# A fixed list of issue orders, DMA transposes and more seven-product batches in a Nystrom attention + MLP kernel

## The chip, the cores and the metric

The kernel runs on one core of a Trainium2 chip. Five engines work side by side, each through its own queue in order: TensorE (PE, with its weight loads, PEld), VectorE (DVE), ScalarE (ACT), GpSimd (POOL) and SyncE (SP, which only issues DMAs here). The metric is the device time of one execution in microseconds. The time before is the median of three runs, 268.52 us (267.44 to 269.39). A profile is one execution of the program, and its span runs from the first to the last instruction.

## The reference

Inputs q, k, v have shape (8 batches, 8 heads, 576 positions, 64). Attention goes through 32 landmarks, each the mean of 18 positions; the result is layer-normed over 512 features and sent through a two-layer MLP (512 to 2048 to 512) with a residual:

```python
q_lm = q.reshape(B, H, m, S // m, D).mean(axis=3)      # m = 32
k_lm = k.reshape(B, H, m, S // m, D).mean(axis=3)
A, Bm, C = sm(q, k_lm), sm(q_lm, k_lm), sm(q_lm, k)    # sm: softmax of scaled products
Z = Bm.transpose(0, 1, 3, 2) / (norm1(Bm) * norminf(Bm) + 1e-06)
for _ in range(6):
    Z = 2 * Z - Z @ Bm @ Z
attn = A @ Z @ C @ v                                    # heads side by side: x, (8, 576, 512)
xn = (x - mean(x)) / sqrt(var(x) + 1e-06) * g_ln
out = x + maximum(xn @ w_ch1, 0.0) @ w_ch2
```

## The kernel before

**Tiling.** A unit is four heads of one batch: a tile of 128 partitions by 1152 values (`stg` as loaded in fp32, `nat` in fp16). Batch 0 is done by `attention0`; the other batches run through `attention2` in the sets (1), (2), (3, 4), (5, 6), (7), whose six iterations of Z share matmuls and banks.

**Turning q and k (batches 1 to 7).** `Coming.turn` makes the transposed tile `xT` with one DVE transpose of 32x32 blocks on pairs of fp16 values (28 of them). The scores therefore run on cells of 32x32 (`scores_k`, `scores_q`: `psec`, `psea`), and the exponentials of the k side, `ec`, are transposed once more on DVE (`ecT`). Landmark sums come in three ways: on TensorE with `pairs16` (`tot`, then the DVE transpose `lmt`), by DVE reductions of `xT` (`add_up`, into `part`), or by sums on POOL (`asum`, `s16`, then `sT`); a matmul with `spread16` brings `part` into the form `lm`. Batch 0 is turned by TensorE with an identity (`pst`, copied to `xT`), and its scores run on 128x64 cells (`psc`) and 64x32 cells (`psa`).

**First layer.** `First.products` multiplies the per-head matrices `zt` with w1 (`m16`, fp16), and `chunk` makes 128 hidden features for 576 positions: four matmuls of 288 columns into one of two double-bank slots (`psh`, tag `p2`), then a ReLU on ACT or DVE into `hT`. The layer norm's mean is taken out of w1 itself: `less` holds minus the mean over features; batches 0 and 1 add it after the product (`copies`, with `less` and `total`), then `center_w1` adds it into w1 for the rest.

**Second layer.** Blocks of 128 positions: 16 matmuls of 512 columns each, then one DVE addition into `xblk` with the norm's factor `rstd`, and two stores. For batches 4 to 7 (`FAST = 4`) four blocks are done by seven products in place of eight (`seven_products`): 112 matmuls of 256 columns in place of 64 of 512, with mixed weights (`w2_mix`, 16 subtractions on POOL), eight mixes of `hT` per batch on DVE (`mix_ahead`) and more, narrower additions.

**What sets the order.** Each engine's order is that in which the program emits. A planner, `Clock`, estimates at build time when each engine and tile is free (`note`, `took`); `run` takes the next ready one of five streams (attentions, totals, first layers, rows of batch 0, second layers), and `help_out` puts loads, casts, mixes, measures and stores between them. A table `AFTER` holds some steps back by count. `Ring` gives out buffers in turn; loads go through six `stg` slots on SP's queue. The first part (batch 0 up to its `zt`, loads and scaling of w1, loads of w2 and of batch 1) is written out by hand.

Of the kernel before, what the change touches and what calls it, by code (L numbers as in the profile page):

```python
# [16 lines left out]
P = 128  # L17
# [3 lines left out]
def kernel(  # L21
# [40 lines left out]
    NEVER = 1e12  # L62

    def name_of(x):
        return x.tensor.name if hasattr(x, "tensor") else x.name

    parted, mixed_, parted_w1 = {}, set(), set()

    def key_of(ap):

        return keys_of(ap)[0]

    def keys_of(ap):
        n = name_of(ap)
        if n not in parted:
            return [n]
        at = [ap.offset]
        for step, k in list(ap.ap)[1:]:
            if step >= parted[n]:
                at = [o + step * i for o in at for i in range(k)]  # L80
        if n in mixed_:
            return [f"{n}:{o // parted[n]}:{int(o % parted[n] >= 256)}" for o in at]
        return [f"{n}:{o // parted[n]}" for o in at]

    class Clock:


        WAY = 55.0
        OVERLAP = {"Activation": 110, "DVE": 80, "Pool": 30}

        def __init__(self):
            self.free = dict.fromkeys(("PE", "DVE", "Activation", "Pool", "SP"), 0.0)
            self.wrote, self.used, self.begun = {}, {}, {}
            self.small, self.lanes, self.wire = False, {}, 0.0
            self.cells, self.count, self.mark, self.fetched, self.ahead = [], 0, 95, 0.0, 0.0
            self.loads, self.pool = [], []
            self.free['PE'], self.issued = 1500.0, 0

        def share(self, span=3400.0):

            now = self.now()
            return sum(c for t, c in self.cells if t > now - span) / span

        def now(self):
            return max([self.free["PE"]] + list(self.lanes.values()))

        BLOCK, LEAD = 128, 16

        def both(self, *at):
            return max(max(at), ps2.next("p2", 2))  # L110

        def calm(self, n):

            return self.fetched if self.count + n + (20 if late() else 0) >= self.mark else 0.0

        def at(self, *tiles):
            return max([self.wrote.get(name_of(t), (0.0, ""))[0] for t in tiles] + [0.0]) + self.WAY

        def at_key(self, ap):
            return self.wrote.get(key_of(ap), (0.0, ""))[0] + self.WAY  # L120

        def idle_key(self, ap):
            n = key_of(ap)
            return max(self.wrote.get(n, (0.0, ''))[0], self.used.get(n, (0.0, ''))[0]) + self.WAY

        def idle(self, *tiles):

            return max([max(self.wrote.get(n, (0.0, ""))[0], self.used.get(n, (0.0, ""))[0],
                            self.begun.get(n, 0.0)) for n in map(name_of, tiles)] + [0.0]) + self.WAY

        def took(self, i, e, n, m):
            op = type(i).__name__
            if e == "Activation":
                return 300 if n < 8 else 190 + (1.07 if name_of(i.outs[0].bass_ap).startswith("ec_") else 0.79) * n
            if e == "Pool":
                if n == 1024 and name_of(i.outs[0].bass_ap) in mixed_:
                    return 2080
                if "Ptr" in op:
                    return 100 + 1.29 * n
                return 100 + 0.92 * n if "Copy" in op else 280 + 1.76 * n  # L140
            if n == 1152 and "Copy" in op:
                return 760
            if "Stats" in op:
                return 690 if m > 100 else 180
            if n >= 512 and (n == 576 or op == 'InstTensorCopy'):
                return 100 + 1.13 * n
            if n == 1024:
                last = max([b for a, b in self.pool if a <= self.ready < b] + [0.0])
                queued = 1000 if self.free["Pool"] > self.ready else 690
                return max(queued, last - self.ready + 560)  # L150
            if n == 256 and "Ptr" in op and name_of(i.outs[0].bass_ap).startswith("xblk"):
                return 480
            if "Transpose" in op:
                return 110 + 1.15 * n
            return 140 + 1.15 * max(n, m if "Reduce" in op else 0)

        def note(self, i):
            e = str(i.engine).rsplit(".", 1)[-1]
            outs = [a.bass_ap for a in i.outs if hasattr(a, "bass_ap")]
            ins = [a.bass_ap for a in i.ins if hasattr(a, "bass_ap")]  # L160
            size = [[k for _, k in a.ap] for a in outs + ins]
            count = []
            for dims in size:
                n = 1
                for k in dims[1:]:
                    n *= k
                count.append(n)
            reads = [n for a in ins for n in keys_of(a)]
            writes = [n for a in outs for n in keys_of(a)]
            ready = 0.0  # L170
            for n in reads:
                t, who = self.wrote.get(n, (0.0, e))
                if who != e or e != "PE":
                    ready = max(ready, t + (self.WAY if who != e else 0.0))
            for n in writes:
                for t, who in (self.wrote.get(n, (0.0, e)), self.used.get(n, (0.0, e)),
                               (self.begun.get(n, 0.0), "")):
                    if who != e:
                        ready = max(ready, t + self.WAY)
            if type(i).__name__ == "InstDMACopy":  # L180
                start = max(self.free[e], ready)
                self.free[e] = start + (580 if e == "SP" else 100)
                half_ = size[0][0] == 64 and any(n.startswith("stg") for n in writes)
                self.wire = (max(start + 1650, self.wire)
                             + count[0] * size[0][0] * 4 / (150.0 if half_ else 385.0))
                self.loads = self.loads[-24:] + [(start, self.wire)]
                self.issued += 1
                late_ = 1500 if self.issued <= 4 else 600 + min(2200, 0.8 * (self.wire - start - 1650))
                done = self.wire + late_
                start = done  # L190
            elif e == "PE":
                cols = count[0]
                if self.count == self.mark - self.LEAD:
                    self.ahead = self.now()
                if self.count == self.mark:
                    self.mark += self.BLOCK
                    ready = max(ready, self.fetched)
                    asked = max(self.ahead, self.fetched - 200)
                    behind = max([w for t, w in self.loads if t <= asked] + [0.0])
                    self.fetched = max(asked + 1200, behind + 400) + 2450  # L200
                self.count += 1
                rows_, cols_ = tuple(i.tile_size)
                self.cells.append((self.now(), cols / 2.4 * rows_ * cols_ / 128 ** 2))
                if tuple(i.tile_size) == (128, 128):
                    if self.small:
                        self.free[e] = max(list(self.lanes.values()) + [self.free[e]]) + 100
                        self.small, self.lanes = False, {}
                    start = max(self.free[e], ready)
                    self.free[e] = start + max(cols / (1.2 if start < 5200 else 2.4) + 3, 56)
                    done = self.free[e] + 160  # L210
                else:
                    if not self.small:
                        self.small, self.lanes = True, {}
                        self.free[e] += 95
                    elif self.shape != (rows_, cols_):
                        self.free[e] = max(list(self.lanes.values()) + [self.free[e]]) + 85
                    self.shape = rows_, cols_
                    lane = [(a, c) for a in range(i.tile_position[0], i.tile_position[0] + rows_, 32)
                            for c in range(i.tile_position[1], i.tile_position[1] + cols_, 32)]
                    start = max([self.free[e], ready] + [self.lanes.get(x, 0.0) for x in lane])  # L220
# [1577 lines left out]
```

## Time and profile before

| | us | how to read it |
|---|---|---|
| runs | 268.52, 267.44, 269.39 | device time of three executions |
| profiled execution, span | 266.1 | first to last instruction; the page does not give this execution's own time, and the median of the runs lies 2.4 above the span |
| granted TensorE clock | 0.999 | full speed throughout |
| chain, TensorE after 45 us | 45 to 262.6 | products of first and second layer, almost without a break |
| start | 0 to 22 | q, k, v and w1 land; batch 0's attention on TensorE between waits |
| last matmul to end | 262.6 to 266.1 | last addition, last store |
| DMA share, 22:45 / 45:85 / 85:150 / 150:240 | 1.05 / 0.93 / 0.60 / 0.17 | loads of weights, then of later batches; stores at the end |
| DVE busy in the same stretches | 16.3 of 23 / 36.9 of 40 / 53.0 of 65 / 67.7 of 90 | |
| ACT busy | 19.3 / 29.2 / 52.2 / 62.0 | |
| POOL busy | 18.8 / 32.1 / 53.6 / 16.1 | casts, sums, mixes of w2; nearly idle after 175 us |

Busy shares are averages over stages with different limits. [...]

### The profile page before, as it was taken

To read this page: it belongs to the slowest core of one execution; us is meant where nothing else is said; L and a number is where in the kernel's file an instruction comes from. 1 tells how busy PE (TensorE), PEld (TensorE's weight loads), DVE (VectorE), ACT (ScalarE), POOL (GpSimd) and SP (SyncE) were. 2 spreads that over 40 slices of the span, in tenths; PEclk is the share of its full clock that TensorE was granted. 3 is DMA by queue.
4 is the path that set the end of the run, shared out by engine and by line. 5 is a ranking of instruction groups with operands and counts; after the bars stand their busy time and mean duration, and the time that the engine had idled before them with its cause. 6 is when DMAs were issued, how large, how long until landed. Compare 5 with 4: busy or idle time off the path is not lost.

```text
span 266.1 us, 8332 instructions
## 1 busy us (share of the span) xinstructions
PE 256.5 (96%) x3442; PEld 167.9 (63%) x3442; DVE 202.8 (76%) x461; ACT 175.2 (66%) x337; POOL 133.6 (50%) x160
## 2 busy tenths in 40 slices
PE   7889998999999999999999999999999999999994
PEld 7644754466545554546655465578878765788883
DVE  2657873899999979788984986989684599819762
ACT  2578997378868896589797559787377654871000
POOL 5288788999729387499999934500000042000000
PEclk9999999999999999999999999999999999999999
DMA  7999999999976996766611120110060006100606
GB/s 253 380 396 389 388 386 393 317 343 306 354 237 172 388 363 187 207 174 198 200 43 39 34 52 2 42 43 0 2 158 0 2 4 160 43 0 2 158 17 183
DMA packets 23566, 46.68 MB, mean 175 GB/s; under 512 B 2404, under 2 KB 2664, under 8 KB 23528
## 3 DMA queue, kind: packets, MB, share of 16 engines
q1 hardware_dynamic: 23048, 45.49, 53.3%
q10 hardware_dynamic: 480, 0.66, 0.7%
q8 instruction: 27, 0.44, 0.7%
q14 instruction: 11, 0.09, 0.1%
HBM read 36.70 MB, written 9.44 MB: 173 GB/s over the span
## 4 chain that ended last, share of the span: by engine, by line
PE 78%; DMA 11%; DVE 3%; POOL 3%; issue 2%; SPq 1%; ACT 1%; POOLq 0%; DVEq 0%
PE bank L304 51%; PE psh L304 21%; DMA stg<-in_v_dram 6%; DMA wstg<-in_moe_w_ch_dram 3%; DMA stg<-in_q_dram 2%; PE pscv L304 1%; POOL natv L298 1%; PE psd L304 1%; DVE xblk L298 1%; PE psec L304 1%; PE psm L304 1%; PE psea L304 1%; POOL w L298 1%; SPq L313 1%; DVE st L298 1%
## 5 line engine op out<-in xcount | busy, mean ns | idle before, releaser
L304 PE MATMUL bank<-w,hT 128*128 128x512 f16 (+3 forms) x528 | 111.7, 335 | 1.2 <-issue 0.8
L298 ACT ACTIVATE hT<-psh 128x576 f16<-128x576 f32 x119 | 73.6, 654 | 21.9 <-PE psh L304 21.0
L304 PEld LDWEIGHTS <-hT 128*128 128x128 f16 x656 | 60.3, 98 | 32.5 <-issue 8.6
L304 PE MATMUL psh<-ea,m 128*128 128x288 f16 x512 | 78.3, 286 | 0.6 <-DVE ea L298 0.3
L304 PEld LDWEIGHTS <-m 128*128 128x128 f16 x512 | 48.8, 97 | 20.2 <-issue 3.7
L298 DVE SCALAR_TENSOR_TENSOR xblk<-bank,rstd,xblk 128x256 f32<-128x256 f32 (+2 forms) x77 | 39.0, 539 | 22.4 <-PE bank L304 22.3
L298 POOL TENSOR_TENSOR ea<-ea,lns 128x576 f16<-128x576 f16 x14 | 18.9, 1371 | 60.4 <-ACT lns L298 54.6
L298 POOL CAST nat<-stg 128x1152 f16<-128x1152 f32 x21 | 23.8, 1147 | 8.5 <-DVE xT L298 6.4
L298 DVE BATCH_NORM_STATS2 six<-xblk 128x6 f32<-128x512 f32 x36 | 24.2, 673 | 0.9 <-ACT xblk L298 0.9
L298 POOL CAST natv<-stg 128x1152 f16<-128x1152 f32 (+1 forms) x17 | 19.3, 1165 | 9.7 <-DMA stg<-in_v_dram 7.7
L298 DVE STREAM_TRANSPOSE xT<-nat 128x576 uint32<-128x576 uint32 x28 | 21.4, 763 | 0.0
L298 ACT COPY xblk<-bank 128x512 f32<-128x512 f32 (+1 forms) x32 | 18.0, 591 | 4.0 <-PE bank L304 3.7
L304 PE MATMUL bank<-w2mix 128*128 128x256 f16 x128 | 17.1, 273 | 0.0
L304 PE MATMUL bank<-w2mix,hT 128*128 128x256 f16 x128 | 15.8, 273 | 0.0
L298 DVE SCALAR_TENSOR_TENSOR st<-st,bank 128x128 f16<-128x128 f16 (+2 forms) x36 | 11.1, 308 | 5.9 <-PE bank L304 5.7
L298 ACT CAST m<-bank 128x512 f16<-128x512 f32 x18 | 9.9, 586 | 7.5 <-PE bank L304 7.4
L298 DVE TENSOR_REDUCE part<-xT 128x32 f16<-128x576 f16 x20 | 14.6, 744 | 0.2
L298 ACT ACTIVATE lns<-psd 128x576 f32<-128x576 f32 x16 | 10.3, 644 | 6.0 <-PE psd L304 5.9
L304 PE MATMUL bank<-zcbd,ea 128*128 128x256 f16 x80 | 14.1, 273 | 0.0
L298 DVE SCALAR_TENSOR_TENSOR m<-less,zsum,bank 128x512 f16<-128x512 f16 (+1 forms) x18 | 11.5, 682 | 3.0 <-PE bank L304 1.4
L304 PEld LDWEIGHTS <-w2mix 128*128 128x128 f16 x128 | 12.4, 98 | 2.0 <-issue 0.2
L304 PEld LDWEIGHTS <-st 32*32 32x32 f16 x448 | 5.9, 90 | 11.9 <-DVE st L298 8.9
(135 smaller groups left out, 365.9 us busy)
## 6 DMA issues: line engine op xcount, KB each, us to landing
stg<-in_q_dram SPq DMA_DIRECT2D x16, 576.0 KB, 6.3
stg<-in_k_dram SPq DMA_DIRECT2D x16, 576.0 KB, 6.0
out_dram<-xblk SPq DMA_DIRECT2D x66, 128.0 KB, 2.4
wstg<-in_moe_w_ch_dram SPq DMA_DIRECT2D x16, 512.0 KB, 7.3
stg<-in_v_dram SPq DMA_DIRECT2D x10, 576.0 KB, 7.2
stg<-in_v_dram SPq DMA_DIRECT2D x6, 288.0 KB, 6.2
stg<-in_v_dram SPq DMA_DIRECT2D x12, 144.0 KB, 6.0
out_dram<-xblk ACTq DMA_DIRECT2D x4, 128.0 KB, 3.2
```

What stands on the lines that cost most here:

```text
L298: return lambda *args, **kw: keep(getattr(self.engine, op)(*args, **kw))
L304: keep(nc.tensor.matmul(o, l, r, start=start, stop=stop, tile_position=(rb, cb), skip_group_check=(skip or cb != 0)))
L313: keep(queue.dma_start(out=t[:], in_=src[b, 4 * u:4 * u + 4].rearrange("(r e) (t j) d -> (e t) r j d", e=2, j=NJ)))
```

## The change

The planner, its `Clock`, the streams and `help_out` are gone. The program now first records all work as operations (`Op`: one instruction, or a run of matmuls), 1656 of them, numbered in the order of the source; then it issues them in the order of a literal list, `ORDER`, with the engine of each movable operation from a second literal, `BY` (A, D or P for ACT, DVE, POOL). Buffers are given out at issue, from fixed slots (`Place`); two psum double banks and four banks as before, `nat` 4 slots (6 before), `e` 12 (14), `mix` 3 and `stg` 6.

- Batches 2 to 7 are turned by a DMA on SP's queue (`turn_by_dma`, 24 in all, 128 x 1152 fp16 each); batch 1 is turned by TensorE as batch 0 is (`BY_PE`). The DVE transposes of `xT`, `ecT`, `sT`, `lmt` and the products with `pairs16` and `spread16` are gone. All scores run on the cells that batch 0 uses (`psc`, `psa`), `psa` of two units together.
- Landmarks: k by POOL sums and a 64-column matmul, q by DVE reductions of the whole `xT` (`qlm`, `HOW`), batch 1 by TensorE.
- `seven_products` for batches 2 to 7; the mixes of `hT` are on DVE or POOL (23 and 25), and each batch uses three `mix` slots.
- Sets are (1), (2), (3), (4, 5), (6, 7). w1 is centred before batch 1's first layer; only batch 0 adds the mean afterwards.
- More casts, ReLUs and scalings may be on DVE or ACT. All loads of v are whole tiles; SP has 70 of the 128 KB stores (66 before).
- Of the hand-written first part the order of loads stays.

```diff
-    class Clock:
...
-    def help_out(hurry=False):
...
-    EARLY = {0: 8}
-    HK, HN, FAST = MCH // 2, DM // 2, 4
...
+    class Op:
+        def issue(self, by):
+            for b in self.bufs:
+                b.place()
+            for ways, args, kw in self.calls:
...
+                    tc.keep_in_program_order(ways(ISSUE[by], *args, **kw))
...
+    def turn_by_dma(n16):
+        t = xT_tile()
+        later("S", lambda e, o, i: e.dma_start_transpose(out=o, in_=i),
+              t, n16.rearrange("p j r d -> p (j r d)"))
+        return t
...
+                xT = [turn_by_pe(t, "AD") if b in BY_PE else turn_by_dma(t) for t in tiles]
...
+    def mix(o, left, right, op):
+        for k in (0, 4):
+            n = ds(k, 4)
+            tt("DP", o[:, n, :], left[:, n, :], right[:, n, :], op)
...
+    SETS = ((1,), (2,), (3,), (4, 5), (6, 7))
+    FAST, BY_PE, TWO = (2, 3, 4, 5, 6, 7), (1,), 2
+    HOW = {(b, nm): "T" if b in BY_PE else "P" if nm == "k" else "D" for b in range(B) for nm in "kq"}
...
+    ORDER = """
+        0-2 14 3-6 9 15 52 17 10 16 18 11 19 55 21 12 20 22-23 58 25 13 24 27 26 28 61 29-30 32 34
...
+    BY = """
+        DADADDPAAAAAADAAAAAADAAADAAAAAADDADAADDADDADDDADADAAADAAAADAAADDAADDDADAADAADPDDPPDPADDP
...
+    for i in order:
+        program[i].issue(by[i])
```

More of the change, by code (lines that the diff above doesn't have):

```diff
@@ L59 @@
     wpool = ctx.enter_context(tc.tile_pool(name="wpool", bufs=1))
[L62 to L83, printed above, removed]
@@ L85 @@
-    class Clock:
[L88 to L220, printed above, removed]
-                    self.lanes.update((x, start + max(cols / 2.4, 30)) for x in lane)
-                    self.free[e] = start + (8 if rows_ == 64 and cols < 128 else 4)
-                    done = self.lanes[lane[0]] + 160
-            else:
-                start = max(self.free[e], ready)
-                self.ready = start
-                done = start + self.took(i, e, count[0], max(count[1:] + [0]))
-                self.free[e] = done - self.OVERLAP[e]
-                if e == "Pool":
-                    self.pool = self.pool[-8:] + [(start, done)]
-                if e == 'DVE' and count[0] == 1024 and writes[0] in parted_w1:
-                    self.free['Pool'] = max(self.free['Pool'], start) + 430
-            for n in reads:
-                self.used[n] = max(self.used.get(n, (0.0, e)), (done, e))
-                if n.startswith("m16") and ":" in n:
-                    self.begun[n[:n.index(":")] + "."] = done
-            for n in writes:
-                self.wrote[n] = max(self.wrote.get(n, (0.0, e)), (done, e))
@@ new lines, with __init__, take @@
+    class Place:
+        def __init__(self, pool, tag, words, slots):
+            self.tag, self.slots = tag, slots
+            self.tiles = [pool.tile([P, words], FP32, name=tag, tag=f"{tag}{i}") for i in range(slots)]
+            self.free = list(range(slots))
+            places[tag] = self
+        def take(self, buf):
+            i = self.free.pop(0)
+            n = 1
+            for d in buf.shape[1:]:
+                n *= d
+            t = self.tiles[i]
+            t = t[0:buf.shape[0], 0:(n if buf.dtype == FP32 else n // 2)]
+            if buf.dtype != FP32:
+                t = t.bitcast(buf.dtype)
+            if len(buf.shape) > 2:
+                names = "abcd"[:len(buf.shape) - 1]
+                spaced = " ".join(names)
+                t = t.rearrange(f"p ({spaced}) -> p {spaced}", **dict(zip(names, buf.shape[1:])))
+            return i, t
@@ new lines, with __init__, take, place @@
+    class Fixed(Place):
+        def __init__(self, tag, tiles):
+            self.tag, self.slots, self.tiles = tag, len(tiles), tiles
+            self.free = list(range(self.slots))
+            places[tag] = self
+        def take(self, buf):
+            i = self.free.pop(0)
+            return i, self.tiles[i][:]
+    class Buf(View):
+        def __init__(self, tag, shape, dtype, name):
+            self.tag, self.shape, self.dtype, self.name = tag, shape, dtype, name
+            self.of, self.chain, self.at, self.uses = self, [], None, 0
+            bufs.append(self)
+        def place(self):
+            if self.at is None and not isinstance(places[self.tag], Turns):
+                self.slot, self.at = places[self.tag].take(self)
+            return self.at
+        def done(self):
+            self.uses -= 1
+            if self.uses == 0 and self.at is not None:
+                places[self.tag].free.append(self.slot)
@@ L431, in load_w1, with e_tile @@
+    def e_tile(shape, name):
+        return Buf("e", shape, FP16, name)
+    less = {}
+    w1_coming, w2_coming = [], []
     def load_w1(i):
         f, half = divmod(i, 2)
-        stg = stage.tile([P, 2, DM], FP32, name="wstg", tag="stg")
-        keep(nc.sync.dma_start(out=stg[:], in_=w1_src[:, 2 * half:2 * half + 2, ts(f, DM)]))
-        w1_coming.append(stg)
-    def scale_w1(i, c, engine):
+        t = Buf("stg", [P, 2, DM], FP32, "wstg")
+        dma(t, w1_src[:, 2 * half:2 * half + 2, ts(f, DM)])
+        w1_coming.append(t)
@@ new lines, with room_for, mean_begun, mean_copied @@
+    hTs = {}
+    def room_for(b):
+        if b < B and b not in hTs:
+            hTs[b] = Buf(f"hT{b % 2}", [P, MCH, S + 64 * (b % 2)], FP16, "hT")
+    def mean_begun(f, psf, c0, c1):
+        for c in range(c0, c1):
+            MM(psf, lesser[:], w1_16[:, c, ts(f, 512)], start=(c == 0), stop=(c == KCH - 1))
+    def mean_copied(f, psf):
+        less[f] = e_tile([P, 512], "less")
+        copy("A", less[f], psf)
+    def center_w1(f):
+        for c in (0, 2):
+            o = w1_16[:, ds(c, 2), ts(f, 512)]
+            tt("D", o, o, less[f][:, None, :].broadcast_to([P, 2, 512]), ALU.add)
@@ new lines, in first_layer, with keep_tail @@
+    def first_layer(l1):
+        two = l1.b >= TWO
+        for m in range(MCH):
+            if two and m % 8 == 0:
+                l1.two_products_of_heads(m // 4)
+            if not two and m % 4 == 0:
+                l1.product_of_heads(m // 4)
+            l1.chunk(m)
+    def keep_tail(b):
+        if b % 2 == 0:
+            room_for(b + 1)
+            copy("P", hTs[b + 1][:, :, 0:64], hTs[b][:, :, S - 64:S])
+    TAIL = {None: ds(0, DM), 0: ds(0, DM - DM // 4), 1: ds(DM - DM // 4, DM // 4)}
@@ L1212, in store @@
+    def store(j, x, cols, last=False):
         for i in range(2):
@@ L1765 @@
     next(a0)
-    run()
-    help_out(True)
+    cut()
+    fixed = len(program)
+    l1, psf = first0[0], {}
+    l1.product_of_heads(0)
+    psf[1] = bank()
+    mean_begun(1, psf[1], 0, KCH)
+    mean_copied(1, psf[1])
+    next(a0)
+    for m in range(MCH):
+        l1.chunk(m)
+        if m in (1, 3):
+            scale_w1(m + 4, 1, "A")
+        if m in (2, 5):
+            f = 2 if m == 2 else 3
+            psf[f] = bank()
+            for c in range(KCH):
+                mean_begun(f, psf[f], c, c + 1)
+                cut()
+            mean_copied(f, psf[f])
+        if m in (1, 4, 7):
+            l1.product_of_heads((m + 2) // 3)
@@ L1771 @@
+    assert sorted(order) == list(range(len(program)))
+    ways = iter("".join(BY.split()))
+    by = [op.by if len(op.by) == 1 else next(ways) for op in program]
+    for i in order:
+        program[i].issue(by[i])
 _INS = ['q', 'k', 'v', 'moe_g_ln', 'moe_w_ch1', 'moe_w_ch2']
```

1901 lines of the change are left out of this document (694 added, 1207 removed), and 38 rows, old and new, of tables (AFTER, ORDER).

## The prediction

> **What bounds the kernel now.** I read the busy times and the chain of waits first.
>
> ```profile
> PE 256.5 (96%) x3442; PEld 167.9 (63%) x3442; DVE 202.8 (76%) x461; ACT 175.2 (66%) x337; POOL 133.6 (50%) x160
> PE 78%; DMA 11%; DVE 3%; POOL 3%; issue 2%; SPq 1%; ACT 1%; POOLq 0%; DVEq 0%
> PE bank L304 51%; PE psh L304 21%; DMA stg<-in_v_dram 6%; DMA wstg<-in_moe_w_ch_dram 3%; DMA stg<-in_q_dram 2%; PE pscv L304 1%; POOL natv L298 1%; PE psd L304 1%; DVE xblk L298 1%; PE psec L304 1%; PE psm L304 1%; PE psea L304 1%; POOL w L298 1%; SPq L313 1%; DVE st L298 1%
> ```
>
> TensorE carries 78% of the chain; DMA has 11%, all of it before 40 us. A busy matmul row overlaps the next one, so 96% does not yet say that TensorE is full. The timeline of TensorE in the middle of the span says it (start, duration, instruction):
>
> ```profile
> 119.82 0.65 PE L304 MATMUL psh<-ea,m 128*128 128x288 f16 x4
> 120.31 0.38 PE L304 MATMUL bank<-w,hT 128*128 128x512 f16 x1
> 120.53 0.38 PE L304 MATMUL bank<-zcbd,ea 128*128 128x256 f16 x2
> ...
> 123.92 0.59 PE L304 MATMUL bank<-w,hT 128*128 128x512 f16 x2
> 124.44 0.41 PE L304 MATMUL bank<-w,zt 64*32 64x512 f16 x8
> 124.67 0.40 PE L304 MATMUL psm<-w,zt 64*32 64x512 f16 x8
> 125.00 0.67 PE L304 MATMUL psh<-ea,m 128*128 128x288 f16 x4
> ```
>
> From start to start, four 288-column products take 0.49 us (122 ns each) and one of 512 takes 0.216 us. That is the price of an instruction here; its own duration includes the pipeline. Two 512s take 0.43 us, yet 124.44 is 0.52 after 123.92: going from 128x128 cells to 64x32 costs 0.09 us. Over the trace the median of such a change of cell shape is 95 ns, and there are 159 of them. With these prices the starts from 22 us to the last matmul at 262.6 us divide into about 222 us of columns, 12.3 us of shape changes, 4.4 us of waits (gaps over 25 ns) and 2 us of crumbs. So TensorE is full from 22 us on, and only fewer columns, fewer changes of shape or those 4.4 us can pay. Before 22 us it waits for loads; from 262.6 to 266.1 lie the last addition and the last store.
>
> Profiled span 266.1 us; the three runs have a median of 268.5, so 2.4 us are added for what lies around the span.
>
> **The change on TensorE, start-to-start prices.** The built instruction streams give the counts.
> - Seven products for batches 2 and 3: out 128 of 512 columns (128 x 0.216 = 27.6), in 224 of 256 (224 x 0.109 = 24.4): -3.2.
> - Landmarks: out 72 products with `pairs16` (56 ns, 4.0) and 10 with `spread16` (1.1); in 36 + 12 of 64 columns (29 ns, 1.4): -3.7.
> - Batch 1 turned by TensorE: 36 transposes at 56 ns: +2.0.
> - Scores of seven batches: out `psec` 224 (4.4), `psea` 224 (3.4), landmark products 112 (0.7). In `psc` 252 at the 20 ns that batch 0's 36 took (5.0), landmark products (0.3), and `psa` in seven pairs. Batch 0's unpaired tile takes 0.5 us, so 14 x 0.5 = 7.0 bounds it above; a pair uses eight different cells at once, 0.213 + 0.027 = 0.24, so 1.7 bounds it below. I take 2.2, near the eight-cell row (`w,zt` x8: 0.23 from start to start). -1.0.
> - Fewer products for `zt`: -0.3. Changes of shape 159 to 171: 12 x 0.095 = +1.1.
>
> Sum -5.1 us. The two unknowns move it from -5.6 to -0.3.
>
> **What else moves.** *DVE.* Sum of durations now 226 us (counts by mean durations; neighbours overlap, hence 202.8 busy). Out: 28 transposes of `xT` (763 ns, 21.4), 20 reductions to `part` (14.6), `ecT` (6.8), `sT` and its reductions (4.9), `lmt` (1.7), nine of the 32 mixes (6.6), 8 `xblk` of 512 (5.8), 8 `m` with `less` (5.9). In: 28 more `xblk` of 256 (476 ns, 13.3), 14 more `hT` (754, 10.5), 10 casts of `nat` and `natv` (760, 7.6), 10 `ea` scalings (288 columns take 524, so 0.95: 9.5), 12 reductions of 1152 columns that no row shows: 576 take 744, so 0.74 if only the output counted and 1.5 by columns; 1.4 taken, 17.0; smaller copies and masks 10.7. Within 1 us of even, and off the path by the cover above: 45 to 85 us runs with DVE at 36.9 of 40 us and PE at 40.0. *ACT* loses (198 to about 181). *POOL* gains: 25 mixes of 1024 (512 columns: 1.15, so 1.1 by the `hT` copy of 1024 to 2.2; 2.2 taken, 55 us), two landmark sums (5.7), less 8 + 7 casts and ten scalings (31): 138 to about 167, still under 0.7 of the span.
>
> *Centring* of w1 (8 x 0.76 us of DVE) comes before batch 1's first layer instead of behind its products; it has TensorE's 15 to 37 us for cover, and beyond it batch 1's products wait.
>
> *SP.* 24 turns are added, each waiting in SP's order for its tile's cast (DVE, ACT or POOL); queued behind it are the next loads and stores. From the first turn on, the casts of those loads stand 4.6 to 11 us of TensorE's columns behind them in the list, against a landing of 6: the shortest have no cover, but the tiles' first TensorE readers come 8 us or more behind their turns. A turn moves 288 KB and no row shows one. Nearest rows:
>
> ```profile
> stg<-in_q_dram SPq DMA_DIRECT2D x16, 576.0 KB, 6.3
> out_dram<-xblk SPq DMA_DIRECT2D x66, 128.0 KB, 2.4
> stg<-in_v_dram SPq DMA_DIRECT2D x6, 288.0 KB, 6.2
> ```
>
> Below: the lone store's 2.4 us. Above: element by element; a packet of 4 bytes takes 9 ns, and 147,456 elements over 16 engines are 83 us. I take 3 to 6, the rows of like size. In the list, a turn of k is issued 12 to 35 us of columns ahead of its TensorE reader, a turn of q 4.4 to 13.5 ahead of DVE's reduction (eight of twelve 6 or more). So 6 us fit nearly all of it, TensorE reads the q tiles later still, and I cost the turns at nothing. [...]
>
> *The list itself.* Of 126 re-uses of a `psh` slot, 52 leave TensorE under 0.95 us of columns to cover one evacuation (0.65 on ACT, 0.75 on DVE, plus the hand-overs); in the new list 17 do, and the median cover grows from 1.09 to 1.80 us. That can win some of the 4.4 us; fuller ACT and DVE at 110 to 130 us of columns (23.5 and 24.3 us of work in 20) can lose as much. I put the waits at no change. Loads to 45 us keep their order, so what is saved there may not count (up to 0.5).
>
> Forecast: 266.1 - 5.1 = 261.0 span, 263.4 us with the 2.4.
>
> **Rivals.**
> *DVE and POOL in each other's way.* The trace speaks for it:
>
> ```profile
> 216.36 0.68 DVE L298 TENSOR_TENSOR w2mix<-hT 128x1024 f16<-128x1024 f16 x1
> 217.16 1.57 DVE L298 TENSOR_TENSOR w2mix<-w2mix,hT 128x1024 f16<-128x1024 f16 x1
> ...
> 216.72 3.16 POOL L298 TENSOR_TENSOR ea<-ea,lns 128x576 f16<-128x576 f16 x2 [43.98 <-ACT lns L298]
> ```
>
> The same mix takes 0.68 us alone and 1.57 when a POOL operation of two inputs runs; single-input ones (`xT`, `six`) do not lengthen. Of the new list's DVE operations of two SBUF inputs (31 mixes and centrings, 10 scalings), those that meet POOL would lose up to 23 us in all by what POOL has queued at their places: some 5 at 15 to 40 us, where batch 1's first layer waits for the centring, and 6 at 90 to 150, where DVE already has 68 us of work for about 64 us of time (at most 11 us of summed durations fit in 10 us, so 70). Decides where the losses pass the 2 us that are left there: 3 to 8 us come back, 266.4 to 271.4, middle 269. [...]
> *Turns late: slower.* If a turn takes 12 us instead of 6, each of six batches holds DVE at its first q reduction about 6 us beyond the cover, and `xblk` and `hT` queue behind it: 36 us, of which DVE's idle time from 45 to 150 us (15 of 105) takes up 15. 263.4 + 21 = 284. Decides above some 8 us. Against it: the landings above, and a quarter of DMA's time is free there.
> *Start-up and loads set the end*, so fewer columns only make TensorE wait: DMA's 11% of the chain is for it, 200 us of full TensorE behind it against. About 267.
> *The turn is element-wise*: 24 x 83 us, 2 ms.
>
> **Chances.** Forecast 0.60; DVE and POOL 0.22; turns late 0.12; loads 0.05; element-wise 0.01. The waits can at most vanish with 1 us of start-up: 258.4, and an under-costed row lowers it by 0.9: 257.5. Upward, to leave out no more than 2 in 10, all of the port rival and the near end of the late turns: 273. The forecast's own range is 257.5 to 265.8. Measurement tells about 1% (2.7 us) from no change: faster (under 265.8) 0.60; same, two thirds of the port case plus the loads, 0.20; slower, the rest, 0.20.
>
> **What would show it.** Right: matmuls 3442 to 3307; the starts divide into about 6 us less of columns, 171 changes of shape at 95 ns, and waits of 3 to 6 us; `psa` pairs near 0.3 us; turns landing within 6 us. [...] Late turns: DVE idle before `qlm` released by a DMA. Wrong at the root: TensorE no longer on most of the chain after 45 us.

## The result, and the profile after

The changed kernel takes 276.10 us (median of four executions, 274.76 to 277.41), the kernel before 268.22: 1.0291 times as long, interval 1.0248 to 1.0333. The forecast was 263.4 us, 257.5 to 273.0: wrong in sign, and outside the range. The profiled execution took 274.76 us, with a span of 273.0. Some executions of a kernel take over 1.5% longer than its fastest one, and the ratios leave these out.

Busy times and the chain of waits of the changed kernel:

```profile
PE 255.4 (94%) x3307; PEld 179.1 (66%) x3307; DVE 214.5 (79%) x442; ACT 167.1 (61%) x294; POOL 172.4 (63%) x174
PE 65%; DVE 11%; DMA 9%; POOL 5%; issue 4%; SPq 1%; ACT 1%; DVEq 0%; POOLq 0%
PE bank L188 41%; PE p L188 23%; DMA stg<-in_v_dram 5%; DMA stg<-in_moe_w_ch_dram 3%; POOL asum L208 2%; DVE nat L195 2%; SPq L225 1%; DVE m L195 1%; DMA out_dram<-xblk 1%; DVE six L520 1%; DVE w L208 1%; DVE e L208 1%; DVE xblk L211 1%; POOL natv L195 1%; POOL mix L208 1%
```

TensorE has 3307 matmuls, as forecast, but 65% of the chain and no longer 78%; DVE went from 3% to 11%, and POOL's sums of k (`asum`) and DVE's casts of `nat` stand in it with 2% each, where they had no line before. "Busy" at 94% hides this, since a TensorE row lasts longer than it costs (four 288-column products of the prediction's lines last 0.65 us and take 0.49 from start to start). The distances from start to start, divided as in the prediction (whole span, us), show where the time went:

| | before | after | difference |
|---|---|---|---|
| columns | 234.6 | 229.6 | -5.0 |
| changes of cell shape (159, 171) | 14.4 | 15.5 | +1.1 |
| waits over 25 ns | 10.4 | 18.9 | +8.5 |
| crumbs | 1.4 | 1.8 | +0.3 |
| last matmul's start to the end | 3.8 | 5.7 | +1.9 |
| span (with 1.5 before the first start) | 266.1 | 273.0 | +6.9 |

The work saved is real. After 22 us the waits rose from 4.4 to 12.8 us, which is 8.4 of the 8.5. Three kinds of loss show in the traces: two among these waits, and the third in what lies behind the last matmul.

**Behind POOL.** Timelines of POOL, DVE and TensorE at 53 us (start, duration, instruction, in brackets the idle time before it and what ended it):

```profile
53.08 1.79 POOL L208 TENSOR_TENSOR e<-e,lns 128x576 f16<-128x576 f16 x1
```
```profile
53.66 1.83 DVE L208 TENSOR_TENSOR e<-e,lns 128x576 f16<-128x576 f16 x1
```
```profile
55.55 0.39 PE L188 MATMUL bank<-zcbd,e 128*128 128x256 f16 x2 [1.01 <-DVE e L208]
```

The same DVE scaling takes 0.75 us where no POOL operation runs beside it. Here it ends 0.6 us after POOL's, and TensorE waits 1.2 us for it, from start to start (the 1.01 in brackets counts from the modelled end of the matmul before).

**Behind the head of a queue.** POOL's timeline ahead of the longest wait of all, 2.1 us at 152.9:

```profile
144.03 2.13 POOL L208 TENSOR_TENSOR mix<-hT 128x1024 f16<-128x1024 f16 x1 [4.57 <-ACT hT L204]
146.10 1.14 POOL L195 CAST nat<-stg 128x1152 f16<-128x1152 f32 x1
147.32 1.48 POOL L208 TENSOR_TENSOR asum<-nat 128x512 f32<-128x512 f16 x1
...
154.30 0.82 POOL L208 TENSOR_TENSOR s<-asum,nat 128x128 f16<-128x128 f32 x1
```

POOL stands idle 4.6 us for ACT's last ReLU, because the mix is next in its order. The cast behind it has had its data since 142.4, and TensorE waits for the `s` at the end. DVE shows the same at 17 us, one place of the list's first part that I had not looked at:

```profile
17.21 0.79 DVE L208 TENSOR_TENSOR e<-e,lns 128x288 f16<-128x288 f16 x1 [2.00 <-ACT lns L199]
17.92 0.27 DVE L211 SCALAR_TENSOR_TENSOR st<-st,bank 128x128 f16<-128x128 f16 x1
```

The scaling waits 2.0 us for ACT; the iteration of Z behind it was ready (with the scaling behind it in `iter_first` below, this wait is gone), and TensorE idles 1.6 us.

**Behind a store.** The issues of SP and of ACT's queue at the end:

```profile
262.87 7.60 SPq L225 DMA_DIRECT2D out_dram<-xblk  x10
```
```profile
267.69 1.20 ACTq L225 DMA_DIRECT2D out_dram<-xblk  x2
```

Ten of the last twelve stores are in one queue at about 0.8 us of issue each; the kernel before had six in each of two:

```profile
257.88 5.62 SPq L1216 DMA_DIRECT2D out_dram<-xblk  x6
257.89 5.89 ACTq L1216 DMA_DIRECT2D out_dram<-xblk  x6
```

### The profile page after: what moved, and what is told of

Same layout as the page of the kernel before. It is cut to its first block, busy times and chain, and to the rows that moved or that the text cites. A ratio compares the mean times of both kernels' runs of the same rounds, so it can differ in the third digit from the quotient of the medians.

```text
span 273.0 us, 8074 instructions
## 1 busy us (share of the span) xinstructions
PE 255.4 (94%) x3307; PEld 179.1 (66%) x3307; DVE 214.5 (79%) x442; ACT 167.1 (61%) x294; POOL 172.4 (63%) x174
## 2 busy tenths in 40 slices
DMA packets 51789, 53.75 MB, mean 197 GB/s; under 512 B 30628, under 2 KB 30888, under 8 KB 51752
## 3 DMA queue, kind: packets, MB, share of 16 engines
q1 hardware_dynamic: 51592, 53.10, 71.6%
## 4 chain that ended last, share of the span: by engine, by line
PE 65%; DVE 11%; DMA 9%; POOL 5%; issue 4%; SPq 1%; ACT 1%; DVEq 0%; POOLq 0%
PE bank L188 41%; PE p L188 23%; DMA stg<-in_v_dram 5%; DMA stg<-in_moe_w_ch_dram 3%; POOL asum L208 2%; DVE nat L195 2%; SPq L225 1%; DVE m L195 1%; DMA out_dram<-xblk 1%; DVE six L520 1%; DVE w L208 1%; DVE e L208 1%; DVE xblk L211 1%; POOL natv L195 1%; POOL mix L208 1%
## 5 line engine op out<-in xcount | busy, mean ns | idle before, releaser
L204 ACT ACTIVATE hT<-p 128x576 f16<-128x576 f32 x105 | 67.2, 655 | 37.8 <-PE p L188 36.9
L188 PE MATMUL bank<-w,hT 128*128 128x256 f16 (+3 forms) x496 | 89.2, 311 | 0.1
L188 PE MATMUL p<-e,m 128*128 128x288 f16 x512 | 79.9, 286 | 0.2 <-ACT m L195 0.2
L205 DVE TENSOR_SCALAR hT<-p 128x576 f16<-128x576 f32 x23 | 17.1, 749 | 11.7 <-PE p L188 11.6
L188 PE MATMUL bank<-stg,mix 128*128 128x256 f16 x192 | 25.6, 273 | 0.0
L208 POOL TENSOR_TENSOR hT<-hT 128x1024 f16<-128x1024 f16 x7 | 16.3, 2334 | 13.7 <-DVE mix L208 13.6
L199 ACT ACTIVATE e<-p 128x576 f16<-128x576 f32 x32 | 19.8, 651 | 8.3 <-PE p L188 7.1
L188 PEld LDWEIGHTS <-mix 128*128 128x128 f16 x192 | 18.1, 98 | 4.6 <-issue 1.6
L208 POOL TENSOR_TENSOR asum<-asum 128x256 f32<-128x256 f32 (+1 forms) x24 | 15.7, 656 | 1.5
L749 DVE TENSOR_REDUCE qlm<-xT 128x64 f16<-128x1152 f16 x12 | 16.0, 1337 | 0.0
```

Of the source, the lines that this page charges most:

```text
L188: PE(lambda e, o, l, r: e.matmul(o, l, r, start=start, stop=stop, tile_position=(rb, cb), skip_group_check=(skip or cb != 0)), o, l, r)
L199: later("A", lambda e, o, i: e.activation(o, i, func, **kw), o, i)
L204: later(by, lambda e, o, i: e.activation(o, i, AF.Relu) if e is nc.scalar else e.tensor_scalar(out=o, in0=i, scalar1=0.0, scalar2=None, op ...
L205: e.tensor_scalar(out=o, in0=i, scalar1=0.0, scalar2=None, op0=ALU.max), o, i)
L208: later(by, lambda e, o, x, y: e.tensor_tensor(out=o, in0=x, in1=y, op=op), o, x, y)
L749: later("D", lambda e, o, i: e.tensor_reduce(out=o, in_=i, axis=AX.XY, op=ALU.add), t[:, x, :], xT[x].rearrange("p j (g a) -> p g j a", a=2))
```

## The experiments

Waits are TensorE's after 22 us in the profiled execution (12.8 in the changed kernel, 4.4 before); ratios are to the kernel before.

**The turns.** Plain copies in place of the 24 turns.

```diff
-        later("S", lambda e, o, i: e.dma_start_transpose(out=o, in_=i),
-              t, n16.rearrange("p j r d -> p (j r d)"))
+        later("S", lambda e, o, i: e.dma_start(out=o, in_=i),
+              t, n16.rearrange("p j r d -> p j (r d)"))
```

> Edit: each of the 24 turns is a plain copy of the same 288 KB from SBUF to SBUF on the same queue at the same place; the turning of the q and k tiles of batches 2 to 7 is left out, all else is computed as before. In the changed kernel SP needs 1.96 us (median) to issue a turn, it lands after 6.3, packets under 512 B rise from 2404 to 30628, and TensorE waits 12.8 us after 22 us (4.4 in the kernel before). Theory A (the turns' hold on SP's queue and on DMA makes a good part of the new waits, since the loads behind them are issued late): SP's issue falls to about 0.4 us, the copies land in 2 to 4 us, DMA's share at 85 to 150 us falls from 1.08 to about 0.7, TensorE's waits after 22 us fall by 3 us or more, and the span by as much. [...]

Measured: 275.76 us, 1.0284 (1.0222 to 1.0346); waits 13.3; the wait near 153 us still 2.1. SP's issue fell from 1.96 to 0.50 us (medians). The landing, from the list of DMA issues of both kernels (count, size where it is given, median us to landing; the load of q beside it took 6.3 before):

```profile
stg<-in_q_dram SPq DMA_DIRECT2D x16, 576.0 KB, 5.9
...
xT<-nat SPq DMA_TRANSPOSE x24, 6.3
```
```profile
xT<-nat SPq DMA_DIRECT2D x24, 288.0 KB, 5.4
```

Windows of both kernels, the changed one first (length, busy times, granted clock, DMA share, GB/s):

```profile
85.00:150.00 65.00, 63.43 (x947) 43.18 (x940) 57.48 (x117) 49.13 (x88) 51.36 (x48) 1.00 1.08 266
```
```profile
85.00:150.00 65.00, 62.88 (x944) 42.76 (x937) 58.65 (x116) 48.83 (x87) 50.95 (x46) 1.00 0.80 254
```

Theory A fails: a quarter of DMA's load (1.08 to 0.80 at 85 to 150 us) and three quarters of SP's issue time go away, and TensorE does not notice (waits 13.3 for 12.8). The copies still land after 5.4 us, so this tells what the turning adds, not what 24 more DMAs cost.

**The tail.**

```diff
-            dma(to, half, "A" if last and i else "S")
+            dma(to, half, "A" if j >= NBLK - 5 and i else "S")
```

> Edit: the second halves of batch 7's last five blocks are stored by ACT's queue, as the kernel before had it; all else as in the changed kernel. In the changed kernel 5.8 us lie between the last matmul and the end, 3.6 in the kernel before. Theory (SP's queue makes the tail: ten stores of 0.6 to 0.8 us each stand in it at the end, two on ACT's): the tail goes back to 3.4 to 4.2 us, the span falls by 1.5 to 2.2 us to about 271, the ratio to the kernel before from 1.029 to about 1.022. Rival (the last addition and the landing of the last store make it): tail 5.3 us or more, time unchanged within 0.5 us.

Measured: 276.11 us, 1.0292 (1.0234 to 1.0349). The tail went from 5.7 to 4.15 us as the theory has it, but not the time. The slices of granted clock (40 equal parts of the span, tenths) of the changed kernel and of this one say why:

```profile
PEclk9999999999999999999999999999999999999997
```
```profile
PEclk9995999999999999999999979999999999999999
```

In this execution TensorE's clock stood at 0.5 from 20.1 to 26.9 us and from 160.1 to 163.5, at most 3.4 and 1.7 us of lost work. That may hide a gain of 1.5 us, but executions of like clock do not show one: 275.36 us at 0.985 against 276.01 at 0.986, yet 275.06 at 0.993 against 274.76 at 0.995. So the shorter tail is shown, a shorter time is not. The kernel before shows no such stretch ahead of its last matmul, and a mean clock of 0.997 to 1.0 in its executions; the changed kernel's four are at 0.979 to 0.996.

**When the clock falls.** In the profiles of these experiments each of eleven stretches of half clock begins during a wait of TensorE of 1.4 us or more, or at most 1.7 us behind its end. The two that follow move the waiting at 17 us, one way and the other.

```diff
-        106 108-109 54 112 110 114 56 68 111 57 144 113 59 71 116 119 115 117 122 60 118 120 123 126
-        124 121 62 125 73 127 129 128 130-132 134 138 64 145 133 135 151 136 141 65 139 137 150 162
+        106 108-109 54 112 110 114 56 68 111 57 113 59 71 116 119 115 117 122 60 118 120 123 126
+        124 121 62 125 73 127 129 128 130-131 144 132 134 138 64 145 133 135 151 136 141 65 139 137 150 162
```

> Edit: one scaling of batch 0's exponentials on DVE (288 columns) is issued behind the last of the six iterations of Z and no longer ahead of the third, as the kernel before has it; all else as in the changed kernel. In the changed kernel this scaling waits 2.0 us for ACT's reciprocals at 17 us, the iteration is queued behind it, TensorE stands idle 1.3 to 1.8 us, and in about half of the executions (mean granted clock 0.98 in place of 0.995) TensorE's clock is then at 0.5 from about 20 to 26 us, which the kernel before never shows. Theory (that idle time lets the clock fall): the wait at 16.5 us falls under 0.4 us, no stretch of half clock is left in any of the six runs (all clocks 0.99 or more), and the median falls from 276.1 to 273.5 to 275. Rival (the clock falls for another cause, such as the loads' landing): clocks of 0.98 stay in some of the runs, the median within 0.7 us of 276.1.

Measured: 275.85 us, 1.0303 (1.0277 to 1.0329); clocks 0.985 to 0.997 over six executions. The 1.6 us at 16.5 us are gone, but 0.8 us of them come back at 20.1, where TensorE waits for the scaled w1. The time is the rival's.

In the next one, operation 131, the second scaling, stands beside 144 ahead of 113.

```diff
-        106 108-109 54 112 110 114 56 68 111 57 144 113 59 71 116 119 115 117 122 60 118 120 123 126
-        124 121 62 125 73 127 129 128 130-132 134 138 64 145 133 135 151 136 141 65 139 137 150 162
+        106 108-109 54 112 110 114 56 68 111 57 144 131 113 59 71 116 119 115 117 122 60 118 120 123 126
+        124 121 62 125 73 127 129 128 130 132 134 138 64 145 133 135 151 136 141 65 139 137 150 162
```

> Edit: the dose the other way: a second scaling of 288 columns is put ahead of the third iteration beside the first; else as in the changed kernel. Theory (idle time of TensorE at 16.5 us lets its clock fall): the wait grows from 1.6 to about 2.0 us, and the half clock comes in all or nearly all runs (mean clock 0.985 or less), median 277 to 278.5. Rival (another cause): clocks mixed as in the changed kernel, median 276.1 plus at most 0.5.

Measured: 277.33 us, 1.0349 (1.0315 to 1.0384); the wait 2.1 us; clocks 0.980 to 0.986 in all four. Its windows show the fall after each of its two long waits (17.0 to 19.0, and 2.1 us at 153.9):

```profile
16.00:20.00 4.00, 1.90 (x65) 1.07 (x63) 2.05 (x6) 1.79 (x4) 3.77 (x5) 1.00 1.05 394
20.00:23.00 3.00, 2.84 (x45) 0.97 (x45) 2.44 (x8) 2.16 (x6) 2.31 (x4) 0.60 1.05 383
...
156.00:162.00 6.00, 5.91 (x63) 4.02 (x63) 5.50 (x9) 3.05 (x6) 5.82 (x4) 0.72 1.03 154
```

So the half clock goes with the long waits: mean clocks of 0.980 to 0.986 with the longer one at 17 us, 0.985 to 0.997 with it gone. That this is worth more than about 1 us of the median is not shown.

**One queue, one instruction.**

```diff
+    for i in (831,):
+        by[i] = "D"
     for i in order:
```

> Edit: one operation of 1024 columns, the second half of the first sum of hT for batch 4's seven products, is on DVE and not on POOL. In the changed kernel POOL stands idle 4.5 us before it (until 144.0 us), waiting for ACT's last ReLU of that layer, and behind it in POOL's order are the cast and the k sums of batch 7, which TensorE reaches at 152.9 and gets at 155.1. Theory (the queue behind a waiting instruction): POOL casts the k tile as soon as it has landed at 142.4, the sums are done 2 us or more earlier, TensorE's wait there falls from 2.1 to under 1 us and the span by 1 to 2 us. Rival (the late load of the other k tile, landed at 145.6 and cast by ACT at 148.8 to 150.0, sets the sums): the wait stays at 1.3 us or more, the span within 0.8 us.

Measured: 1.0303 (1.0218 to 1.0388), from two of four executions (275.03 and 278.30 us; the others took 279.75 and 280.66): no gain is seen, and one of 1 us could not be. In the profiled execution, the one of 279.75 us, the wait for `s` fell from 2.1 us to 0.7, but POOL's cast and sums, now earlier, run beside DVE's other mixes: two of those take 1.63 us in place of 0.68, the moved one follows them, the iteration of Z stands behind it, and TensorE waits 2.4 us at 147.

**Four unblocked queues together.** The scaling as in the first of the two above; 230 behind 279; 1297 ahead of 831; the stores as in the tail's experiment.

```diff
-        160 87 226 180 161 223 209 230 278 224 78 208 193 210 279 213 194 283 227 89 280 181 80 289
+        160 87 226 180 161 223 209 278 224 78 208 193 210 279 230 213 194 283 227 89 280 181 80 289
-        671 814 1282 832 1313 816 815 834 662 821 817 995 255 822 975 996 825 831 976 665 823 1003
-        1005 826 661 1290 1004 1006 997 999 1054 1000 836 1297 1056 1055 827 1058 833 1059 1302 1315
+        671 814 1282 832 1313 816 815 834 662 821 817 995 255 822 975 996 825 1297 831 976 665 823 1003
+        1005 826 661 1290 1004 1006 997 999 1054 1000 836 1056 1055 827 1058 833 1059 1302 1315
```

> Edit: four changes of order or queue on the changed kernel: the scaling behind the iterations; the centring of one part of w1 behind DVE's copy of batch 1's first turned tile (TensorE waits 1.1 us for it at 30.4); the cast of batch 7's k tile on POOL ahead of the mix that waits for ACT until 144.0; the second halves of the last stores on ACT's queue. Theory (the lost time is waits behind instructions at the head of a queue): -0.9 us at 30 us, -1.0 at 153, -1.5 after the last matmul, and the half clock gone: median 271 to 273.5, between the kernel before and the changed one. Rival (each freed wait is met by the next one or by loads): 274.5 or more.

Measured: 274.62 us, 1.0246 (1.0204 to 1.0287); the waits 12.6. The tail is 4.2 us, the wait for `s` 0.65, the one at 30.4 gone. But a wait for batch 1's scores at 33.6 grew from 0.4 to 1.2, and one for `zt` at 157.6 from 0.7 to 0.95. The median is 1.5 us below the changed kernel's, where the theory had 2.6 to 5.1. Mostly the rival: the next wait takes the place of the one removed.

**Work moved between engines.** Two kernels change `by` alone.

```diff
+    for i in (332, 746, 990, 1369, 634, 631, 635, 643, 831, 835, 842, 1110,
+              1109, 1113, 1111, 1112, 1114, 1121, 1122, 1214, 1489, 1491, 1501,
+              1492, 1591, 1588, 1590, 1600, 1601):
+        by[i] = "D"
     for i in order:
```

> Edit: the 25 mixes of hT (1024 columns, some 2.2 us each on POOL) and the four scalings of the exponentials that POOL has are all on DVE; POOL keeps casts, k sums, copies and the mixes of w2. [...]

Measured: 286.60 us, 1.0643 (1.0582 to 1.0704); DVE 227.5 us busy, waits 26.3 (in an execution of 289.55 us with three stretches of half clock). The waits double, and the median is 10.5 us above the changed kernel's: DVE has no room for this work.

```diff
+    for i in (462, 464, 479, 481, 490, 679, 920, 944, 1314, 1325):
+        by[i] = "A"
     for i in order:
```

> Edit: the ten casts of nat and natv that DVE has after batch 0 (758 ns alone, 1428 where POOL adds beside them) are on ACT; else as in the changed kernel. [...] Rival (ACT, whose ReLUs free TensorE's banks, is now late): the waits before the 288-column products grow and the time is 1 us or more longer.

Measured: 278.48 us, 1.0390 (1.0356 to 1.0425). DVE falls by 9 us busy and the waits rise to 16.6: those before the 288-column products from 1.6 to 2.9 us, those before the products with `bones` from 0.3 to 2.0. The rival.

**POOL's work left out.** In place, all but one column of its sums, mixes and scalings; POOL keeps its casts, its copies and the mixes of w2, and every instruction stays in its place in the list:

```diff
     def tt(by, o, x, y, op):
-        later(by, lambda e, o, x, y: e.tensor_tensor(out=o, in0=x, in1=y, op=op), o, x, y)
+        def way(e, o, x, y):
+            if e is nc.gpsimd and not (by == "P" and op == ALU.subtract):
+                o, x, y = (t[tuple([slice(None)] + [slice(0, 1)] * (len(t.shape) - 1))] for t in (o, x, y))
+            return e.tensor_tensor(out=o, in0=x, in1=y, op=op)
+
+        later(by, way, o, x, y)
```

The buffers of sums and mixes are filled with zeros at the start.

> [...]

Measured: 273.59 us, 1.0194 (1.0134 to 1.0254); waits 11.5, those at 153 us and at 54 to 56 gone, a new one of 2.2 us at 126 for a mix. The median is 2.5 us below the changed kernel's.

> The same parts of POOL's work left out, together with the four changes of order and queue of the kernel called unblock above. Theory (POOL, the heads of queues and the stores' queue are the three causes, and they add up): waits after 22 us 4 to 7 us, 4.2 us after the last matmul, a span of 263 to 266 us: about what the forecast had (261.0) plus the 2 to 4 us of waits that are left. Rival (there are further waits of the list itself, without POOL): span 268 us or more.

Measured: 269.71 us, 1.0074 (1.0039 to 1.0108); waits 8.0, span 266.7, between the two spans. The two edits give 2.5 and 1.5 us alone and 6.4 together, as they would if each alone ran into the waits that the other removes.

**Reading or lateness.** On `unblock`, POOL fills its outputs with zeros, twice, for about the same time, and reads nothing:

```diff
+            if e is nc.gpsimd and not (by == "P" and op == ALU.subtract):
+                tc.keep_in_program_order(e.memset(o, 0.0))
+                return e.memset(o, 0.0)
```

> The kernel called unblock above, and each of POOL's k sums, mixes of hT and scalings of the exponentials is two fills of its output with zeros (1024 columns took 0.95 us a fill, so two are near the 2.2 us of a mix): POOL reads nothing for them, is about as busy as in unblock, and the sums, mixes and scalings themselves are left out. Bounds: unblock has 12.6 us of waits after 22 us and a median of 274.6 us, pool_tiny_unblock 8.0 us and 269.7. [...] Rival (POOL's lateness, what waits for its results and stands behind it, is the price): waits 11 us or more, median 273 us or more.

Measured: 271.35 us, 1.0135 (1.0103 to 1.0166), waits 8.9. DVE's groups of the changed kernel and of this one (busy us, mean ns):

```profile
L208 DVE TENSOR_TENSOR e<-e,lns 128x576 f16<-128x576 f16 x10 | 11.2, 1115 | 0.1
...
L208 DVE TENSOR_TENSOR mix<-mix,hT 128x1024 f16<-128x1024 f16 x7 | 7.1, 1016 | 0.0
```
```profile
L212 DVE TENSOR_TENSOR e<-e,lns 128x576 f16<-128x576 f16 x10 | 7.5, 749 | 0.1
L212 DVE TENSOR_TENSOR mix<-mix,hT 128x1024 f16<-128x1024 f16 x7 | 4.8, 682 | 0.0
```

In `unblock` itself the two means are 1088 and 1102 ns. With POOL 155.7 us busy (172.8 in `unblock`) but reading nothing for these operations, DVE's scalings and mixes run at their lone speed, and 3.3 of the 4.9 us between `unblock` and `pool_tiny_unblock` are won. The rival's 11 us of waits and 273 us are not reached. But the fills also relieve POOL's lateness, so how the 3.3 us divide is not shown: two fills of 1024 columns take 1.9 us and a mix 2.2, and a fill waits for no input (in `unblock` POOL stands idle 9.7 us in all ahead of the first additions of the k sums, most of it for casts of `nat`, and not at all ahead of their fills). Not everything of DVE's is free beside a fill, either: two casts of `nat` take 1.18 and 1.01 us there, 0.76 alone.

**What is left.** Two kernels on `pool_tiny_unblock`: the turns as copies again, and the centring of w1 left out but for two columns.

> The kernel called pool_tiny_unblock above, and its 24 turns as plain copies of the same 288 KB (the turning is left out too). In pool_tiny_unblock TensorE still waits 8.0 us after 22 us, 4.4 in the kernel before; in the changed kernel plain copies alone took nothing away (13.3 us of waits against 12.8). Theory (the turns cost nothing even where POOL and the heads of queues no longer cover them): waits 7 to 9 us, span 266 to 267.5. Rival (the turns were covered by the other waits, and the loads behind them on SP's queue make those at 127 to 142 us): waits 6 us or less, span 265 or less.

Measured: 268.63 us, 1.0022 (0.9993 to 1.0050). The waits are 8.6, with a half clock at 8.1 to 15.0 us in the profiled execution; of those at 127 to 142 us one of 0.8 is gone and another is 0.7 for 0.5. By the median the turns cost about 1 us here, but the two intervals overlap and the waits do not place it; I leave it open.

```diff
-            o = w1_16[:, ds(c, 2), ts(f, 512)]
-            tt("D", o, o, less[f][:, None, :].broadcast_to([P, 2, 512]), ALU.add)
+            o = w1_16[:, ds(c, 1), ds(512 * f, 2)]
+            tt("D", o, o, less[f][:, None, 0:2].broadcast_to([P, 1, 2]), ALU.add)
```

> The kernel called pool_tiny_unblock above, and of the eight additions that centre w1 on DVE all but two columns left out (684 ns alone, 1.1 us beside POOL's casts). [...]

Measured: 268.10 us, 1.0008 (0.9979 to 1.0037); the waits at 30 to 40 us 0.5 (from 1.8), and the median 1.6 us lower: batch 1's first layer pays for the centring, 684 ns alone and 1122 on average (675 to 1635) where POOL casts or scales beside it. The profiled span fell by 0.5 us only: waits of 0.55 and 0.94 us are new at 76 and 115 us.

## Why the prediction was wrong, step by step

- **Columns: right in kind, 1.2 us too good.** -6.2 forecast, -5.0 measured. Seven products (27.6 out, 24.4 in), landmarks (-3.7) and batch 1's turning (+2.0) came out to a tenth. The scores gave -0.7 and not -1.0: the 32x32 ones removed had cost 7.2 and not 8.5, the new ones cost 4.2 for `psc` and 2.0 for `psa`, so the guess of 2.2 was good. `zt` gave nothing, and three more matmuls of zeros (`warm`, 56 for 53) cost 0.3; the other 0.3 is not placed.
- **Changes of shape: right**, 12 more, +1.1.
- **"I put the waits at no change": the step that failed.** TensorE's waits after 22 us went from 4.4 to 12.8 us, +8.4. The re-use cover of `psh` that I counted as a possible gain gave none: waits before the 288-column products are 1.6 us, 1.5 before. The list was judged by what stands between a producer and its reader on TensorE. I did not ask, of each engine, which ready instructions stand behind one that waits: the scaling at 17 us, the centring at 30, the mix at 144. "Of the hand-written first part the order of loads stays" made me skip the rest of that part.
- **DVE and POOL in each other's way: the right rival, with too small a chance and too small a price.** Its chances and its range call it the port rival; no run shows a port, they show DVE's operations longer beside POOL's (a mix of 0.68 us up to 2.23). 0.22 and "3 to 8 us come back", 269. DVE's durations sum to 238.7 us, 227 forecast; in `memset_unblock` they are 230.1. The casts, which I priced at 760 ns, count too: one of `nat` takes 758 ns alone and 1428 where POOL works beside it (six of eleven). POOL's single-input casts lengthen the centring as well (1.63 us at 29.1 beside a cast of `nat`, 0.68 alone), against my "when a POOL operation of two inputs runs". Its place at 15 to 40 us was right (`tiny_unblock_center`), its other, at 90 to 150, only in part.
- **The turns cost nothing: right, for a reason that was partly luck.** They land in 6.3 us, a little outside my 3 to 6, and SP needs 1.96 us to issue one, which I had not priced. DVE is never idle before `qlm`, so the late-turns rival is out; without POOL's share they may be worth 1 us.
- **The tail: a step that was missing.** I read the end before as "the last addition and the last store" and left it as it was, though I had counted SP's stores as 70 for 66. +1.9 us, of which `tail_act` takes back 1.5 in the tail itself, though not in its median.
- **Single durations were mostly right:** POOL's mixes at 2.2 us are 2.2 to 2.3, `qlm` at 1.4 is 1.34; POOL's sum, about 167, is 177.5.
- **The 2.4 us outside the span** are 1.8 in the profiled execution; the rest was the spread of the runs.
- **The lower bound has a slip:** 4.4 us of waits and 1 of start-up off 263.4 give 258.0, not 258.4. The measured time lies on the other side.

The sum closes: 263.4 + 1.2 (columns) + 8.5 (waits) + 0.3 (crumbs) + 1.9 (tail) - 0.6 = 274.7, against 274.76. The median lies 1.3 above it: the other three executions have spans of 274.2, 274.4 and 275.7 us at clocks of 0.986, 0.996 and 0.979, and the clock (0.995 in the profiled one) may explain two of them. Of the 8.5 us of waits the experiments account for POOL's two-input work and three changes of order (4.6, whole span) and for the centring (0.5); the other 3.4 us, in waits of 0.9 us and less, stay unassigned. No version of the new list that computes everything beat the kernel before; the best is `unblock` at 274.6 us.

## What to carry to other kernels

Where engines run fixed orders, the cost of an order is at the heads of the queues: list for each engine the instructions that will wait there, and what stands ready behind them, from the first microsecond to the last store. Freeing one such wait in a full schedule mostly exposes the next, so price them together. Before a second engine shares DVE's elementwise work, find each pair of DVE and POOL operations that will run side by side, casts included, and price DVE's by what POOL's still has to run: here a mix of 0.68 us took up to 2.23.

## What the runs showed of the hardware

- **DVE's operations that began beside one of POOL's ended 0.5 to 0.6 us behind it.** In the changed kernel 28 of DVE's casts from fp32 and two-input operations of 576 or 1024 columns are more than 10% longer than alone. Each lasts what POOL's operation in progress still has to run, plus 0.53 to 0.55 us (1024 columns) or 0.61 to 0.62 (576, and the casts): the scaling at 53.66 us is 1.22 + 0.61 = 1.83, a mix at 207.75 is 1.68 + 0.55 = 2.23, a cast at 155.69 is 1.51 + 0.62 = 2.12. The 1.57 us in the prediction's lines is 1.03 + 0.55. Two that started ahead of POOL's or with it were not lengthened: a mix at 103.77, 45 ns ahead of POOL's, takes 0.69 us, and a scaling at 114.20, 14 ns behind POOL's, 0.74. Beside POOL's fills in `memset_unblock` the scalings of 576 columns took 0.75 us and the mixes of the table above 0.68.
- **Half clock came behind some of TensorE's longer waits.** Of some two dozen waits of 1.4 us or more in the profiled executions, 11 were followed by a clock of 0.5, for about 3.4 or 6.8 us (in `tail_act` from 20.1 to 26.9 us and from 160.1 to 163.5); none of the shorter ones was. The changed kernel's own two longest, 1.6 us at 16.5 and 2.1 us at 152.9, were not: its clock is 1.00 from 16 to 30 us and from 150 to 168. What decides between them is not shown. The same program differs from execution to execution, with mean clocks of 0.979 to 0.996 in the changed kernel's four.
- **A DMA transpose was dearer than a copy.** By the queue's share of the span, a turn of 288 KB held the 16 engines 2.24 us ((71.6% of 273.0 - 53.3% of 266.1) / 24); by DMA's shares at 45 to 85, 85 to 150 and 150 to 240 us (1.05, 1.08 and 0.32, with copies 0.83, 0.80 and 0.27) a copy held them 1.3 us less. Packets under 512 B were 30628, 2404 before. The landings differ less, 6.3 us against 5.4.
